# Additive mask bias written into PSUM by an identity product, logits in token order, and a regrouped schedule, in a fused attention and soft-MoE kernel

## Chip, cores and metric

The kernel runs on one core of a Trainium2 chip. The metric is the device time of one execution in microseconds (us); lower is better. Runs are sorted into fast and slow by their time, and each run lists the mean clock that was granted to TensorE (PE), as a share of full speed. Only fast runs are compared. The other engines are VectorE (DVE), ScalarE (ACT) and GpSimd (POOL). SBUF holds the operands here, PSUM (in banks) the sums of the products.

## The reference, cut to what matters

```python
# attention: B, H, S, D = 8, 8, 576, 64; heads 0-3 a plain window, heads 4-7 a dilated one
scores = scale * q @ k.T                           # scale = 1/8
mask_plain = (rel >= 0) & (rel < 32)
mask_dil   = (rel >= 0) & (rel < 128) & (rel % 4 == 0)
attn = softmax(where(mask, scores, -1e9)) @ v      # x: 4608 tokens x 512
# soft MoE: 32 slots, 8 experts of 4 slots, hidden size 1024
logits = x @ phi
slot_input = softmax(logits, axis=tokens).T @ x
slot_out[e] = relu(slot_input[e] @ w1[e]) @ w2[e]
out = softmax(logits, axis=slots) @ slot_out       # needs every expert
```

Inputs and outputs are fp32 in HBM. The loads cast to fp16 on their way into SBUF and the output stores cast back. q, k, v, w1 and w2 are 62 MB, the output 9.4 MB.

## The kernel before

One loop iteration handles one batch element ("a batch" below) and mixes three stages of a pipeline: scores, exponentials and plain products of batch b, dilated products and logits of b-1, slot sums of b-2. After the loop come the experts, which need all weights, and then the outputs, which need all experts. Scores are computed with 32 contraction rows (tiles of 32 rows by 128 columns of PE's 128x128 array, four at a time, one per head); the mask is a product on DVE after the exponential. `keep_busy` issues products with no use ("fillers"), meant to keep the clock of PE up.

```python
def emit_scores(b, st):                    # st 0, 1: plain and left edge; st 2: dilated
    tiles = [psum_s.tile([128, 2, 512], FP32, ...) for i in range(2)]   # 2 banks each
    ...
    for kt_, k0, qt_, q0, c0, w in jobs:
        for tt in range(2):
            for h in range(4):
                nc.tensor.matmul(tiles[h // 2][:, h % 2, c0 : c0 + w],
                    kt_[32 * h : 32 * h + 32, k0 : k0 + 128, tt],
                    qt_[32 * h : 32 * h + 32, q0 : q0 + w, tt],
                    start=(tt == 0), stop=(tt == 1), skip_group_check=True)
    return tiles

def emit_exp(b, st, tiles, i):             # ACT
    nc.scalar.activation(out=pt, in_=tiles[i][:, :, 0:n], func=AF.Exp, scale=SCALE)

def emit_mask(b, st, i):                   # DVE: 480, 304 or 512 columns x 2 heads
    nc.vector.tensor_tensor(out=pt, in0=pt, in1=MASK[st]..., op=ALU.mult)

def back_logits(b, rp, filler):            # rp: two of the four residues mod 4
    keep_busy(bank, filler, 512)
    for kc in range(4):
        if kc < 2:                         # plain half: every 4th column
            rhs = xTp_t[b][:, kc, :].rearrange("p (i r) -> p r i", r=DIL)[:, 2 * rp : 2 * rp + 2, :]
        else:                              # dilated half: contiguous
            rhs = xTd_t[b][:, kc - 2, 2 * rp : 2 * rp + 2, :]
        nc.tensor.matmul(lp, phi4[:, kc]..., rhs, start=(kc == 0), stop=(kc == 3))
    nc.scalar.activation(out=ET[...every 4th column...], in_=lp, func=AF.Exp, scale=1.0)
# ... cut: loads, transposes, products with v, normalisation on DVE, slot sums ...
```

Per batch the loop holds 4,000 columns of fillers: 2x224 after each of two transposes, 3x352 before the third normalisation, 3x512 and 1x512 before the logits.

The softmax here doesn't subtract the row's maximum and nothing guards it: scores larger than these inputs give would overflow.

## Time and profile before

| | before |
|---|---|
| time, median of 3 | 203.08 us (201.67 to 206.15) |
| profiled run | span 213.3 us, a slow run, mean clock 0.776 |
| batch period where the clock is 1.00 | 16.0 us |
| batch period where the clock is lower | 17.6 to 20.4 us |
| fp32 bytes read and written | 62.43 MB and 9.44 MB |

The page of the profile cuts the span into 40 equal slices (5.33 us each here). The digits are tenths: busy share of PE, granted clock, busy share of the DMA engines; the last row is what the DMA engines moved in GB/s, counted as fp16 for loads.

```profile
PE   7724999599988889999898898898689999758800
PEclk9965559955799965555999999999755699995555
DMA  5999999999994996699999999999999800199994
GB/s 120 164 205 208 206 205 212 209 205 165 202 210 64 202 205 120 107 196 212 210 185 198 211 209 207 209 171 181 206 207 207 140 5 0 35 404 406 409 407 114
```

Two things stand out. The clock falls to half, or near it, in stretches of three to five slices, in spite of the fillers. And the DMA engines move at most 205 to 212 GB/s of fp16, which is twice that in fp32 read.

The next view cuts the loop by the first exponential of the dilated scores, so that each row is one batch period. Columns: start and end, length, busy time (and count) of PE, PE weight loads, DVE, ACT and POOL, the granted clock, the DMA share and GB/s.

```profile
core 0: us, PE busy (x) PEld busy (x) DVE busy (x) ACT busy (x) POOL busy (x), PEclk, DMA share, GB/s
...
63.62:81.23 17.61, 15.91 (x271) 10.67 (x271) 14.65 (x37) 10.46 (x17) 7.00 (x8) 0.87 0.96 162
81.23:101.60 20.37, 20.37 (x271) 13.51 (x272) 14.18 (x34) 10.75 (x17) 7.42 (x9) 0.53 0.92 156
101.60:117.61 16.01, 14.23 (x271) 9.38 (x271) 13.88 (x35) 10.47 (x18) 10.12 (x12) 1.00 1.17 199
117.61:133.58 15.97, 14.21 (x271) 9.36 (x270) 13.87 (x35) 10.45 (x17) 3.49 (x4) 1.00 1.17 209
...
```

The run is slow, so its total is not compared with anything; the rows at clock 1.00 are. In such a row neither PE nor DVE is full by itself: they wait for each other. The timeline of these two rows (start, length, engine, line, operation, output<-inputs, partitions and elements, and in brackets the idle time before and what ended it) shows where, first for DVE and then for PE:

```profile
110.87 0.65 DVE L309 TENSOR_TENSOR p_0_0_1982<-p_0_0_1982,masks 128x960 f16<-128x960 f16 x1
...
112.53 0.67 DVE L309 TENSOR_TENSOR p_0_1_2001<-p_0_1_2001,masks 128x960 f16<-128x960 f16 x1
...
113.33 0.78 DVE L380 TENSOR_TENSOR rc_9_2074<-rc_9_2074,masks 128x4 f32<-128x4 f32 x1
```

```profile
114.63 0.28 PE L327 MATMUL o_1_2171<-v_93,p_0_0_1982 128*128 128x128 f16 x2 [0.28 <-DVE xd_2008 L381]
...
116.28 0.28 PE L327 MATMUL o_2_2187<-v_93,p_0_0_1982 128*128 128x128 f16 x2 [0.37 <-DVE xp_2167 L381]
...
120.19 0.81 PE L161 MATMUL lg_0_2286<-ones 128*128 128x512 f16 x3 [0.54 <-ACT xTd_2240 L417]
```

DVE spends 3.1 us of the 16 on six such mask products (by their start-to-start times) and 0.8 on one more small product, and PE waits for DVE's normalisations to free its output buffers. A filler of 512 columns costs PE 0.21 us.

### The profile page before, as it was taken

The page shows a single profiled execution, that of the slowest core. Times are in us where ns is not written, and L with a number is a line of the kernel's source. Part 1 is how long each engine was busy: PE and PEld are TensorE (multiplying, and loading weights), DVE is VectorE, ACT ScalarE, POOL GpSimd, SP SyncE. Part 2 cuts the span into 40 slices and gives each one's busy share as a digit, 9 for nine tenths or more (in the row PEclk, how much of TensorE's full clock was granted, in tenths as well). Part 3 has the DMA queues.
Part 4 walks back from the last instruction along what each step waited for, and adds up shares of the span by engine and source line. Part 5 has one row for each costly group of instructions (what it writes and reads, how often), then busy time and mean ns, then how long its engine had stood idle before and what let it go on. Part 6 is the DMA issues. An engine that isn't in the chain of part 4 may idle for free.

```text
span 213.3 us, 5627 instructions
## 1 busy us (share of the span) xinstructions
PE 173.7 (81%) x2410; PEld 102.3 (48%) x2410; DVE 133.5 (63%) x320; ACT 100.2 (47%) x160; POOL 86.5 (41%) x120
## 2 busy tenths in 40 slices
PE   7724999599988889999898898898689999758800
PEld 2312645474765566477556556556447554311100
DVE  3476892958599686668969969948225012545630
ACT  2033332553837825462783783784432502545520
POOL 7555644604441640633179005066200000297960
PEclk9965559955799965555999999999755699995555
DMA  5999999999994996699999999999999800199994
GB/s 120 164 205 208 206 205 212 209 205 165 202 210 64 202 205 120 107 196 212 210 185 198 211 209 207 209 171 181 206 207 207 140 5 0 35 404 406 409 407 114
DMA packets 32617, 41.27 MB, mean 193 GB/s; under 512 B 2128, under 2 KB 19664, under 8 KB 32592
## 3 DMA queue, kind: packets, MB, share of 16 engines
q0 software_dynamic: 32160, 40.41, 103.1%
q1 hardware_dynamic: 432, 0.50, 0.9%
q8 instruction: 19, 0.31, 0.5%
q14 instruction: 6, 0.05, 0.1%
HBM read 62.43 MB, written 9.44 MB: 337 GB/s over the span
## 4 chain that ended last, share of the span: by engine, by line
PE 49%; DVE 17%; DMA 9%; issue 9%; ACT 8%; POOL 4%; POOLq 0%; ACTq 0%
DMA raw_1_137<-in_k_dram 6%; POOL out_dram L770 4%; DMA raw_0_121<-in_q_dram 3%; PE warm_454 L161 3%; ACT ET L434 2%; PE so L725 2%; DVE qk_91 L258 2%; ACT v_93 L228 2%; DVE qk_90 L258 1%; DVE xd_2008 L381 1%; DVE xd_869 L381 1%; DVE xd_520 L381 1%; DVE xd_2381 L381 1%; PE hps_3298 L698 1%; PE hps_3299 L698 1%
## 5 line engine op out<-in xcount | busy, mean ns | idle before, releaser
L161 PEld LDWEIGHTS <-ones 128*128 128x128 f16 x138 | 12.4, 108 | 18.6 <-issue 10.8
L770 POOL DMA_DIRECT2D out_dram<-ot_3468 x1 | 0.6, 566 | 34.6 <-ACT ot_3468 L765 34.6
L431 PEld LDWEIGHTS <-phi_62 128*128 128x128 f16 x64 | 7.6, 119 | 9.1 <-issue 3.3
L290 PEld LDWEIGHTS <-qk_90 32*128 32x128 f16 x416 | 7.0, 103 | 10.0 <-issue 3.8
L762 PEld LDWEIGHTS <-ET 128*128 128x128 f16 x36 | 3.6, 99 | 15.4 <-issue 14.1
L161 PE MATMUL warm<-ones 128*128 128x512 f16 x26 | 7.5, 458 | 1.5 <-DVE ones L512 1.5
L290 PEld LDWEIGHTS <-qk_91 32*128 32x128 f16 x416 | 6.5, 98 | 3.0 <-issue 2.4
L161 PE MATMUL warm_454<-ones 128*128 128x512 f16 x20 | 5.8, 460 | 0.0
L487 DVE TENSOR_TENSOR UT<-UT,u_3264 128x160 f32<-128x160 f32 x1 | 0.3, 322 | 8.1 <-PE u_3264 L478 8.1
L304 ACT ACTIVATE p_0_0_238<-s_0_0_212 128x960 f16<-128x960 f32 x1 | 1.0, 972 | 9.1 <-PE s_0_1_213 L290 9.1
L205 PEld LDWEIGHTS <-onehot 32*128 32x128 f16 x128 | 3.3, 108 | 3.9 <-issue 3.4
L234 POOL COPY v_93<-vs_1950 128x1024 f16<-128x1024 f16 x1 | 1.0, 1037 | 9.8 <-PE o_8_2412 L327 9.8
L290 PE MATMUL s_1_0_245<-qk_90 32*128 32x16 f16 (+3 forms) x24 | 1.1, 208 | 4.6 <-DVE qk_90 L267 3.5
L214 PEld LDWEIGHTS <-onehot 16*128 16x128 f16 x32 | 3.8, 119 | 1.2
L251 POOL DMA_DIRECT2D w_3_2704<-in_moe_w_dram x1 | 0.9, 878 | 8.5 <-DVE qk_91 L267 8.5
L258 DVE STREAM_TRANSPOSE qk_90<-raw_0_121 128x576 uint32<-128x576 uint32 x1 | 1.3, 1258 | 4.8 <-DMA raw_0_121<-in_q_dram 4.8
L242 POOL COPY v_93<-v_93 32x1024 f16<-32x1024 f16 x4 | 4.1, 1034 | 0.2
L242 POOL COPY v_92<-v_92 32x1024 f16<-32x1024 f16 x4 | 4.1, 1034 | 0.2
L175 POOL DMA_DIRECT2D raw_6_1566<-in_q_dram x1 | 0.7, 696 | 8.5 <-DVE qk_90 L267 8.5
L175 POOL DMA_DIRECT2D raw_4_808<-in_q_dram x1 | 0.7, 701 | 7.9 <-DVE qk_90 L267 7.9
L478 PEld LDWEIGHTS <-ones 128*128 128x128 f16 (+1 forms) x40 | 3.4, 97 | 0.7 <-issue 0.7
L251 POOL DMA_DIRECT2D w_7_2833<-in_moe_w_dram x4 | 2.8, 717 | 2.0 <-ACT xTp_2776 L404 2.0
(1101 smaller groups left out, 658.2 us busy)
## 6 DMA issues: line engine op xcount, KB each, us to landing
w_0_76<-in_moe_w_dram POOLq DMA_DIRECT2D x1, 1024.0 KB, 16.7
w_1_77<-in_moe_w_dram POOLq DMA_DIRECT2D x1, 1024.0 KB, 18.9
w_2_78<-in_moe_w_dram POOLq DMA_DIRECT2D x1, 1024.0 KB, 12.8
w_3_79<-in_moe_w_dram POOLq DMA_DIRECT2D x1, 1024.0 KB, 12.9
w_4_80<-in_moe_w_dram POOLq DMA_DIRECT2D x1, 1024.0 KB, 12.8
w_5_81<-in_moe_w_dram POOLq DMA_DIRECT2D x1, 1024.0 KB, 17.0
w_6_82<-in_moe_w_dram POOLq DMA_DIRECT2D x1, 1024.0 KB, 12.5
w_7_83<-in_moe_w_dram POOLq DMA_DIRECT2D x1, 1024.0 KB, 17.2
```

The costliest lines, as they stand in the source:

```text
L161: nc.tensor.matmul(dst, ones[:, 0:128], ones[:, 0:width], start=True, stop=True, skip_group_check=True)
L214: nc.tensor.matmul(tiles[0][:, 0, 1, :], onehot[0:LEFT, r, :], vl[0:LEFT, 0:4, D * r : D * r + D], start=False, stop=(r == DIL - 1), skip_ ...
L228: nc.scalar.copy(out=dst[:, :, :, 0:D], in_=src.rearrange("p t (h d) -> p t h d", h=4))
L242: nc.gpsimd.tensor_copy(out=vL[b % NV][0:32, :, :, 0:D], in_=vD[b % NV][96:128, :, :, 0:D])
L258: nc.vector.transpose(out=dst, in_=src)
L290: nc.tensor.matmul(tiles[h // 2][:, h % 2, c0 : c0 + w], kt_[32 * h : 32 * h + 32, k0 : k0 + 128, tt], qt_[32 * h : 32 * h + 32, q0 : q0 + ...
L381: nc.vector.tensor_tensor(out=dst.rearrange("p (u d) -> p u d", u=4), in0=o[0:nq, :, 0:D], in1=rc[0:nq, :, None].broadcast_to([nq, 4, D]), ...
L431: nc.tensor.matmul(lp, phi4[:, kc].rearrange("p c s -> p (c s)"), rhs, start=(kc == 0), stop=(kc == 3))
L434: nc.scalar.activation(out=ET[:, b * S : b * S + S].rearrange("p (i r) -> p r i", r=DIL)[:, 2 * rp : 2 * rp + 2, :], in_=lp, func=AF.Exp, ...
L698: nc.tensor.matmul(hps[fc][32 * j : 32 * j + 32, :], siTm[:, dc, e, :], w1t[e][:, dc, 512 * fc : 512 * fc + 512], start=(g == 0 and dc == ...
L725: nc.tensor.matmul(so[32 * j : 32 * j + 32, :], hTm[g][:, c, 32 * j : 32 * j + 32], w2t[4 * g + j][:, c, :], start=(seen[j] == 0), stop=(s ...
L770: nc.gpsimd.dma_start(out=out[r0 : r0 + 128, :], in_=ot)
```

## The change

The intent is to take the mask off DVE. A product of the 128x128 identity with a table of 0 and -60000 writes the bias into the score banks first, and the scores accumulate on it; after the scale of 1/8 the exponential of a masked score is 0. The Trainium skill, "PSUM — Partial Sum Buffer" (The four PSUM rules), names this way of starting an accumulation from a value: put the seed through the PE by an identity product. The PE time for it is to be paid by dropping the fillers in the loop and by an explicit order of operations that changes the tile size of the array less often (15 changes per batch). The logits now run in token order, the last 64 rows of v come by a DMA of their own instead of a permuting product, one of two v evictions moves from ACT to DVE, and the first-layer weights are issued somewhat earlier. The small product with `mask_ok` (the 0.8 us on DVE) is dropped too.

```diff
+FAR = -60000.0
-    m.append(ok)
-    return np.ascontiguousarray(np.concatenate(m, axis=1).astype(np.float16))
+    return np.ascontiguousarray(np.where(np.concatenate(m, axis=1), 0.0, FAR).astype(np.float16))
+ORDER = """
+SA D0 nD0 XP0 eXP0 eA1 D2 XP1 loads D3 eA0 nD2 EP ER nD3 QP0 DL last eXP1 D1 SB eB0 nDL nD1
+P1 VS eB1 U P2 UA R2 R1 QD00 nP1 nP2 SC eC0 eC1 P0 nP0 XD0 XD1 eXD0 QP1 P3 eXD1 P4 R3 R4
+QD01 VP VE0 VE1 QD10 LG0 LG1 nP3 ET0 ET1 nP4 QD11
+"""
     def emit_scores(b, st):
+        n, m0 = WIDTH[st], BIAS0[st]
+        for h in range(4):
+            nc.tensor.matmul(
+                tiles[h // 2][:, h % 2, 0:n], ident, bias[:, m0 : m0 + n],
+                start=True, stop=False, skip_group_check=True)
...
-                        start=(tt == 0),
+                        start=False,
-    def emit_mask(b, st, i):
...
-        keep_busy(bank[:, 288:512], 2, 224)        # and the other fillers of the loop
...
-                rhs = xTp_t[b][:, kc, :].rearrange("p (i r) -> p r i", r=DIL)[:, 2 * rp : 2 * rp + 2, :]
+                rhs = xTp_t[b][:, kc, n * hf : n * hf + n]
-                rhs = xTd_t[b][:, kc - 2, 2 * rp : 2 * rp + 2, :]
+                rhs = xTd_t[b][:, kc - 2].rearrange("p r i -> p i r")[
+                    :, n // DIL * hf : n // DIL * (hf + 1), :]
...  (cut: v tail by its own DMA, evictions, weight issue (1,1,1,1,2,2) -> (2,1,2,1,1,1))
```

In ORDER, S is scores, eA to eC their exponentials (ET those of the logits; eX are evictions of transposes), P and D products with v of the same block (plain, dilated), R products with the block before (32x32 array tiles), n normalisations, X transposes, LG logits, EP and U the slot sums, QP and QD transposes of q and k, VP and VE the permutation and eviction of v. Each engine runs its own items in that order.

## The prediction

> **What bounds it now.** The profile is of a slow run (213.3 us, mean granted clock 0.776); the timed runs are at 203.08. In the chain of waits the eight batches repeat. From mask to mask a batch takes 15.99 us at clock 1.00 (110.95 to 126.95, 126.95 to 142.94), and 17 to 19.6 where the clock row shows 0.5 to 0.8; those excesses sum to about 9.5 us, so I take the timed runs as mostly warm. In a warm batch (timeline) DVE has one hole, about 1.6 us, before the first dilated normalisation; PE stands idle about 1.4 us (0.16, 0.28, 0.37, 0.54), each time for DVE or ACT. The chain hops between PE and DVE; neither alone is the bound. After the loop: row sums, experts, then outputs at 406 GB/s, about 27 us from the first (184) to the end. Loads run at 205 to 212 GB/s and end near 170 in this slow run: a second limit not far below.
>
> **Costs per warm batch, by start-to-start times in the timeline.**
> - DVE loses six mask products (0.57, 0.60, 0.39, 0.39, 0.59, 0.60 = 3.1 us) and the validity product (0.8), and gains one V eviction (0.5 to 0.6): 14.4 us of work becomes about 11.1.
> - PE gains 12 identity products, 4x(480+304+512) = 5,184 columns. The warm 512-column filler is 0.21 us apart, so 2.15 us. It loses fillers of 4,000 columns (1.65 us), the 16-row permutation (0.45), and tile-size switches: I count 23 before and 15 after. A switch costs 0.1 us beyond a matmul (114.80 to 114.96 against 0.055), 0.8 us together. "TensorEngine Tiling (Array Packing)" of the Trainium skill (Key Properties) says changing the tiling mode drains the engine; the trace agrees. Strided logit operands (0.25 us a matmul against 0.18 contiguous here) move from the plain to the dilated half: a wash. PE work goes from 14.6 to about 13.8 us.
> - ACT loses one V eviction (0.5), and the exponentials of the logits write contiguously (0.8 us now for 288 columns, about 0.45 expected): 10.4 becomes about 9.
> - POOL issues one more small DMA (0.55 us); not critical.
>
> **What reaches the time.** With the masks gone the products wait for ACT alone, and PE becomes the leading engine; its remaining waits (buffers of the outputs, the copies before the logits) I put at 0.5 to 0.9 us. A batch takes about 14.4 us, 1.6 less. Seven repeat fully: 11 us. The first batch gains 1 to 2, because the second transpose of batch 1, which waits for k until 21.5 us, now stands behind three normalisations. The last back end and the fillers of the warm-up change by under 1 us. The limit from loads: 62.4 MB read at about 415 GB/s of fp32 is 150 us, plus the last expert pieces and 27 us of output: about 184. Sum: 203 - 11 - 1.5 - 1 = about 189.5.
>
> **Prediction: 189 us, 8 in 10 between 183.5 and 197.** Faster by over 2%: 0.90; within 2%: 0.07; slower: 0.03.
>
> **What would show it.** Batch period 14 to 15 us at clock 1.00; DVE busy per period about 10.5 to 11.5 against 13.9, with new holes; identity products about 2.1 us a batch at 0.2 us each; logit exponentials near 0.45 us; no fillers in the middle and a granted clock no lower; gap between last load and first output shrunk.
>
> **What would make it wrong.** A clock that falls to half without the fillers: then a batch takes 18 us and the gain is gone. The strided dilated logits costing more than 0.3 us each. Identity products that wait for score buffers, putting evictions on PE's path. Loads: if a batch nears 14 us the last weights set the end and nothing below 184 is reachable.

## The result, and the profile after

| | before | after |
|---|---|---|
| time, median | 204.62 us of 4 (201.67 to 210.81) | 190.73 us of 4 (190.48 to 191.67) |
| ratio of fast runs | | 0.943 (95%: 0.936 to 0.951) |
| mean clock, profiled run | 0.776 (slow run) | 0.880 (fast run) |
| batch period at clock 1.00 | 16.0 us | 14.0 us |
| DVE busy in it | 13.9 us | 10.7 us |

A ratio is the mean time of one kernel's fast runs over that of the other's fast runs of the same rounds, so it is not quite the ratio of the medians: here 190.9 over 202.4, the mean of 201.67 and 203.08. The other two runs of before are slow. The outputs are right.

The page after, in slices of 4.72 us:

```profile
PE   6951999999999999999999998998899957869300
PEclk9995557999999999999999999999985999975555
DMA  5999999999999999999999999999999990999992
GB/s 136 191 203 209 203 205 205 211 213 206 205 212 206 206 215 209 206 208 209 205 209 212 201 211 209 203 208 209 205 208 208 208 167 15 302 408 403 409 407 76
```

After the first batch the clock stays up (1.00 in the six batch periods after the first, 0.84 in the first; it dips again in the last iteration, which has no scores), and the DMA row has no hole between the first slice and the one at 15 GB/s: the loads run at their highest rate from start to end. The chain of waits, followed back from the last instruction, goes over loads nearly everywhere:

```profile
DMA 76%; POOL 9%; issue 8%; DVE 2%; PE 1%; POOLq 0%; ACT 0%; DVEq 0%
```

The same batch windows as before:

```profile
core 0: us, PE busy (x) PEld busy (x) DVE busy (x) ACT busy (x) POOL busy (x), PEclk, DMA share, GB/s
...
70.66:84.67 14.01, 13.79 (x269) 8.98 (x268) 10.73 (x28) 8.93 (x16) 4.14 (x6) 1.00 1.20 208
84.67:98.67 14.00, 13.78 (x269) 8.97 (x268) 10.74 (x28) 8.94 (x17) 7.25 (x10) 1.00 1.20 208
...
```

PE now leads: it is busy for 13.8 of 14.0 us, DVE for 10.7. In the timeline of a batch, the identity products, the logits and their exponential:

```profile
96.96 0.60 PE L282 MATMUL s_2_0_2174<-bias,ident 128*128 128x512 f16 x2
97.41 0.59 PE L282 MATMUL s_2_1_2175<-bias,ident 128*128 128x512 f16 x2
...
101.35 0.42 PE L452 MATMUL lg_0_2282<-xTp_1977,phi_62 128*128 128x288 f16 x2
101.61 1.14 PE L452 MATMUL lg_0_2282<-xTd_2236,phi_62 128*128 128x288 f16 x2
102.57 0.42 PE L452 MATMUL lg_1_2287<-xTp_1977,phi_62 128*128 128x288 f16 x2
```

From 96.96 to the first score at 97.93 the four identity products of 512 columns take 0.97 us; the other two groups take 0.92 and 0.77 (a wait of 0.22 left out), so 2.66 us per batch with the entry to the scores, against 2.15 predicted. The logits hold a surprise: from 101.35 to 101.61 two contiguous products take 0.26 us, and from 101.61 to 102.57 two strided ones take 0.96 us, or 0.48 us each.

After the loop, PE waits for the last expert weights, though the loads never paused:

```profile
152.68 0.38 PE L746 MATMUL so<-w_6_2734,hslab 128*32 128x512 f16 x1 [0.72 <-DMA w_6_2734<-in_moe_w_dram]
153.94 0.38 PE L746 MATMUL so<-w_7_2782,hslab 128*32 128x512 f16 x1 [0.88 <-DMA w_7_2782<-in_moe_w_dram]
155.19 0.38 PE L746 MATMUL so<-w_7_2782,hslab 128*32 128x512 f16 x1 [0.63 <-DMA w_7_2782<-in_moe_w_dram]
```

So the time seems to have moved from one limit to another: from an attention loop that PE and DVE shared, with a clock that fell, to a loop led by PE that ends just before the loads do. Every part of that sentence can be tested, and was.

### The profile page after: what moved, and what is told of

It is laid out like the page before. It is cut to its first block, busy times and chain, and to the rows that moved or that the text cites. A ratio compares the mean times of both kernels' runs of the same rounds, so it can differ in the third digit from the quotient of the medians.

```text
span 188.9 us, 5560 instructions
## 1 busy us (share of the span) xinstructions
PE 158.4 (84%) x2392; PEld 88.9 (47%) x2392; DVE 109.6 (58%) x287; ACT 87.2 (46%) x152; POOL 90.1 (48%) x128
## 4 chain that ended last, share of the span: by engine, by line
DMA 76%; POOL 9%; issue 8%; DVE 2%; PE 1%; POOLq 0%; ACT 0%; DVEq 0%
DMA w_7_2782<-in_moe_w_dram 14%; DMA w_2_86<-in_moe_w_dram 13%; DMA w_2_78<-in_moe_w_dram 11%; DMA vs_1258<-in_v_dram 11%; DMA raw_7_1992<-in_q_dram 10%; DMA vs_147<-in_v_dram 6%; DMA vs_135<-in_v_dram 4%; DMA out_dram<-ot_3501 3%; DMA out_dram<-ot_3546 2%; DMA out_dram<-ot_3441 2%; POOL out_dram L791 1%; POOL v_93 L236 1%; POOL v_93 L240 1%; POOL v_93 L244 1%; POOL vs_562 L199 0%
## 5 line engine op out<-in xcount | busy, mean ns | idle before, releaser
L282 PEld LDWEIGHTS <-ident 128*128 128x128 f16 x96 | 8.8, 101 | 18.1 <-issue 13.2
L170 PEld LDWEIGHTS <-ones 128*128 128x128 f16 x56 | 6.2, 118 | 10.5 <-issue 6.1
L452 PEld LDWEIGHTS <-phi_62 128*128 128x128 f16 x64 | 6.1, 101 | 9.4 <-issue 7.6
L170 PE MATMUL warm<-ones 128*128 128x512 f16 x26 | 8.5, 503 | 1.5 <-DVE ones L541 1.5
L302 PEld LDWEIGHTS <-qk_90 32*128 32x128 f16 x416 | 6.1, 98 | 4.9 <-issue 4.9
L302 PEld LDWEIGHTS <-qk_91 32*128 32x128 f16 x416 | 5.6, 92 | 4.3 <-issue 4.3
L253 POOL DMA_DIRECT2D w_7_2782<-in_moe_w_dram x4 | 2.8, 711 | 7.1 <-DMA w_2_86<-in_moe_w_dram 4.4
L170 PE MATMUL rs<-ones 128*128 128x448 f16 x10 | 4.3, 569 | 0.0
L746 PEld LDWEIGHTS <-hslab 128*32 128x32 f16 x64 | 1.7, 95 | 4.9 <-issue 3.7
L282 PE MATMUL s_1_1_294<-bias,ident 128*128 128x304 f16 x2 | 0.7, 434 | 4.0 <-DVE v_92 L229 4.0
L746 PE MATMUL so<-w_7_2782,hslab 128*32 128x512 f16 x8 | 2.4, 379 | 1.7 <-DMA w_7_2782<-in_moe_w_dram 1.5
```

The lines of the kernel that those rows point to most:

```text
L170: nc.tensor.matmul(dst, ones[:, 0:128], ones[:, 0:width], start=True, stop=True, skip_group_check=True)
L253: nc.gpsimd.dma_start(out=w2t[e][:, n * i : n * i + n, :], in_=src[:, n * i : n * i + n, :])
L282: nc.tensor.matmul(tiles[h // 2][:, h % 2, 0:n], ident, bias[:, m0 : m0 + n], start=True, stop=False, skip_group_check=True,)
L302: nc.tensor.matmul(tiles[h // 2][:, h % 2, c0 : c0 + w], kt_[32 * h : 32 * h + 32, k0 : k0 + 128, tt], qt_[32 * h : 32 * h + 32, q0 : q0 + ...
L452: nc.tensor.matmul(bank[:, 0:n], phi4[:, kc].rearrange("p c s -> p (c s)"), rhs, start=(kc == 0), stop=(kc == 3),)
L746: nc.tensor.matmul(so[32 * j : 32 * j + 32, :], hTm[g][:, c, 32 * j : 32 * j + 32], w2t[4 * g + j][:, c, :], start=(seen[j] == 0), stop=(s ...
```

## The experiments

The main theory (A): moving the masks off DVE and the dense schedule are both needed; the identity products cost PE what they save DVE unless fillers, waits and switches are taken out. Rivals: DVE alone was the bound (B); the fillers alone cost the time (C); the order alone gains it (D). Twelve kernels ran, on three chips. On the first chip the kernel before had a median of 207.88 us, on the second 207.0, on the third 205.56, because many of its runs there were slow (mean clock 0.78 to 0.88; fastest run 200.6). So a ratio depends on the runs of before that it is set against: the same two kernels give 0.943 in the result and 0.927 in e8. Ratios are given where enough fast runs of both exist.

### e1: identity products in the kernel before

```diff
 # kernel before, emit_scores: bias products first, scores accumulate; all mask products dropped
+        for h in range(4):
+            nc.tensor.matmul(tiles[h // 2][:, h % 2, 0:n], ident, masks[:, m0 : m0 + n], start=True, ...)
-                        start=(tt == 0),
+                        start=False,
-            emit_mask(b, 0, 0)     # and the five others
```

Expected: 

> The kernel before with one part of the change: identity products write the bias, the mask products on DVE are gone; order, fillers, logits as before. Theory A (the gain comes from order, switches and fillers, which only pay for the identity products): PE work per warm batch goes from about 13.4 us (16.0 less 2.6 of waits) to about 16.1, so the period cannot fall: 16.2 to 17.5 us, time 203 to 213. Theory B (DVE was the bound and moving the masks off it is the gain): period about 14.5, time about 192.

Measured: 204.38 us median (fast runs 203.41 to 204.65), ratio 0.992 (0.980 to 1.004), unclear at best. Two of its batch periods (the profiled run, 207.96 us, counts as slow, but these rows are at clock 1.00):

```profile
46.93:63.72 16.79, 15.83 (x284) 10.26 (x283) 11.36 (x28) 10.54 (x17) 6.70 (x8) 1.00 0.98 164
63.72:80.34 16.62, 15.66 (x284) 10.35 (x283) 10.78 (x28) 10.55 (x17) 6.70 (x8) 1.00 1.02 170
```

Theory A is kept, B falls: taking 2.5 us of work off DVE made the warm period longer, 16.6 to 16.8 instead of 16.0. But the clock reads 1.00 in all six periods after the first one, which the kernel before does not reach. The fast runs have a mean clock of 0.906 to 0.924, those of before on this chip 0.82 to 0.855: the steadier clock seems to give back about what the longer period costs.

### e2 and e3: fillers out, with and without the identity products

```diff
-        keep_busy(bank[:, 288:512], 2, 224)
-                keep_busy(ubank[:, 160:512], 3, 352)
-        keep_busy(bank, filler, 512)
```

Expected of e2 (e1 without the loop's fillers): 

> As e1, and the fillers in the loop are gone too. Theory A: PE work about 14.3 us and waits of 1 to 1.8 left by the old order: period 15.3 to 16, time 196 to 203. Theory B: 190 to 192, all of the gain. If the clock falls without fillers, time above 205 with PE clock 0.5 stretches.

Measured: 199.52 us median (196.62 to 202.03), ratio 0.962 (0.940 to 0.984). Periods at clock 1.00 are 15.5 and 16.0 us, those at 0.90 are 16.6.

```profile
43.43:58.91 15.48, 14.13 (x273) 9.43 (x271) 10.76 (x28) 10.54 (x17) 6.70 (x8) 1.00 1.20 208
58.91:75.50 16.59, 15.27 (x273) 10.01 (x271) 11.01 (x28) 10.54 (x18) 6.70 (x8) 0.90 1.11 189
```

That is A's range: identity products paid by the fillers gain part of the whole change (ratio 0.962 against 0.943 or 0.927), though at the 2% threshold unclear. PE still stands idle 1.35 us of the 15.48, and the clock dips. What separates e2 from the kernel after is the order together with the logits, the v tail, the v eviction and the dropped small product; these were not taken apart further than e9 and e10 do.

Expected of e3 (kernel before, only the fillers taken out): 

> The kernel before without the fillers in the loop, nothing else. Theory A: the fillers stand partly in PE's waits for DVE, so taking away 1.76 us of them shortens the warm period by less than 0.6 us (15.4 to 16.0), and the clock falls to 0.5 more often: time 203 to 215. Theory C (the fillers themselves cost the gain): period 14.3, time about 191.

Measured: 208.45 us median (204.51 to 212.0); only one of its four runs counts as fast, so no ratio. The mean clock of its runs is 0.66 to 0.73. One of its periods (in a slow run):

```profile
82.47:100.68 18.21, 17.71 (x260) 12.50 (x260) 14.16 (x35) 10.55 (x18) 7.64 (x9) 0.50 0.92 154
```

C falls: without fillers and without identity products PE has less work than in before, e1 or e2, and runs it at a lower clock. What the fillers were worth in the kernel before is not shown: the one fast run (204.51 us) lies with the fast runs of before on this chip (204.83 to 207.88).

### e4 and e5: masks back on DVE in the kernel after, then with the identity products kept as dead weight

```diff
 # e4: kernel after, ORDER gets mask products (mA..mC), no identity products
-... nD3 QP0 DL ...   nP1 nP2 SC ...            QD01 VP VE0 VE1 QD10 ... nP4 QD11
+... nD3 QP0 mA1 mA0 DL ... nP1 nP2 mB0 mB1 SC ... QD01 VP VE0 VE1 mC0 QD10 ... nP4 mC1 QD11
 # e5: as e4, but the 12 products of ident and the 0/1 table stay; the scores overwrite them
-                        start=False,
+                        start=(tt == 0),
```

Expected of e4: 

> The changed kernel with the mask products back on DVE and no identity products; everything else of the change kept. PE work per batch about 10.6 us, DVE about 14.2. Theory A (both parts are needed: PE paid by order, DVE relieved by the bias): DVE leads, period 14.3 to 15.7, time 193 to 201. Theory D (the order is all, the bias gives nothing): 188 to 191, equal to the changed kernel. A clock that falls without dense products shows as 0.5 to 0.8 in the clock row and more than 200.

Measured: 206.36 us median (205.64 to 207.73), ratio 1.004 (0.993 to 1.015): the whole gain is gone. This missed the range of A (193 to 201) and lies where the expectation put a fallen clock. The mean clock is 0.70 to 0.72:

```profile
61.69:80.42 18.73, 16.14 (x256) 11.81 (x256) 14.89 (x35) 8.94 (x16) 8.19 (x9) 0.59 1.18 209
80.42:96.12 15.70, 13.78 (x256) 9.79 (x257) 13.78 (x35) 8.94 (x17) 7.32 (x9) 0.83 1.14 186
```

Is that the clock, or DVE? e5 keeps PE's load as in the kernel after and DVE's as in e4. Expected: 

> As e4 (mask products on DVE in the changed kernel), but the identity products stay on PE at their old size and place, without effect: the scores overwrite them. PE work is that of the changed kernel, DVE that of e4. e4 ran at a mean clock of 0.70 to 0.72 and gained nothing. Theory E (the identity products' use is twofold: DVE relief and a clock that stays at 1.00): clock back at 1.00 in the loop, period 14.9 to 16 set by DVE, time 196 to 203. Theory F (e4 lost by the clock alone, DVE relief is worth nothing): time 190 to 192. Theory G (e4 lost by DVE alone): time stays at 204 to 208.

Measured: 202.75 us median (201.7 to 204.89), ratio 0.981 (0.970 to 0.993), inside E's range of time, but not its clock: E had 1.00 throughout the loop.

```profile
63.37:78.24 14.87, 13.79 (x268) 8.96 (x268) 13.38 (x34) 8.93 (x17) 7.50 (x9) 1.00 1.13 212
78.24:95.22 16.98, 15.89 (x268) 10.04 (x268) 14.36 (x36) 8.93 (x17) 7.32 (x9) 0.83 1.24 206
```

At clock 1.00 the period is 14.9 us, about 0.9 us more than in the kernel after: PE does the same work (13.8 us) and waits 0.86 us at one place for a normalisation on DVE. The rest comes from periods like the second line: while PE waits for DVE, the clock dips although all the dense products are there. From e4 to e5 the products are worth about 4 us (on two chips, so only roughly), and from e5 to the kernel after, with DVE relieved, another 11 (fast runs 201.7 to 203.25 against 190.85 to 191.67, same chip). D falls: the order without bias and without fillers gains nothing (e4), and with dead products in the place of fillers little (e5); the order with the old fillers was not run. F and G fall too.

### e6, e7, e8: loads, fillers, control

```diff
 # e6: experts 6 and 7 use the second-layer weights of 4 and 5 (wrong on purpose): 4 MB less in SBUF
-            load_w2(6)
+            w2t[6] = w2t[4]
-            load_w2(7, 4)
+            w2t[7] = w2t[5]
 # e7: fillers back, before each half of the logits
+        keep_busy(bank, 4, 512)
 # e8: the kernel after, unchanged
```

Expected of e6: 

> The changed kernel without the last two 2 MB weight loads (experts 6 and 7 use the second-layer weights of 4 and 5: wrong result on purpose). The loads then end about 10 us earlier. PE waited for the last weights for 0.7 + 0.9 + 0.6 + 0.3 us in the tail. Theory H (loads and computation end together): 188 to 189.3, a gain of 1.5 to 3 us and no more. Theory I (bound by loads throughout, as the chain of waits reads): about 181. Theory J (bound by computation, the loads merely abut): 190.5 to 191.

Measured: 186.42 us median (185.19 to 186.97), a wrong result as intended. Against e8 on the same chip (191.24) that is 4.8 us less. This is more than H's 1.5 to 3 us, and half of what I (bound by loads throughout) claimed; J (no gain) falls as well. The tail shows most of it: from the last slot sums on DVE to its copy of the slot outputs the kernel after takes 14.8 us (143.99 to 158.78), e6 11.1 us (142.62 to 153.72), with no wait for weights. First the kernel after, then e6:

```profile
143.99 0.32 DVE L516 TENSOR_TENSOR UT<-UT,u_3212 128x160 f32<-128x160 f32 x1 [7.88 <-PE u_3212 L507]
158.78 0.42 DVE L770 CAST so_sb<-so 128x256 f16<-128x256 f32 x1 [1.51 <-ACT so_sb L769]
142.62 0.32 DVE L516 TENSOR_TENSOR UT<-UT,u 128x160 f32<-128x160 f32 x1 [7.89 <-PE u L507]
153.72 0.42 DVE L768 CAST so_sb<-so 128x256 f16<-128x256 f32 x1 [1.01 <-ACT so_sb L767]
```

So loads cost 3.7 us at the end, not the 2.5 that the single waits sum to. Without these two loads the computation sets the end, 4 to 5 us earlier. A chain that reads "DMA 76%" did not mean that 76% of the time could be saved there.

Expected of e7: 

> The changed kernel with 4 fillers of 512 columns before each half of the logits, 4,096 columns or 1.75 us of PE work per batch, about what the kernel before had. If PE is the engine that sets the 14.0 us period: period 15.4 to 15.8, and with 2 us of slack in front of the last loads, time 198 to 202. If loads set the period: 14.0 to 14.3, time 190.5 to 192.

Measured: 196.71 us median (196.58 to 200.16; one of five is slow). PE sets the period:

```profile
57.85:73.58 15.73, 15.51 (x277) 9.76 (x276) 10.72 (x28) 8.93 (x17) 7.30 (x9) 1.00 1.20 209
```

The period grew by 1.72 us for 1.75 us of fillers, so there is no slack for fillers in the loop. The total grew by 5.5 us, less than the 7 or more expected (198 to 202 us). The trace shows where the difference went: from the last slot sums to the slot outputs e7 takes 9.9 us (158.01 to 167.94), against 14.8 in the kernel after. It no longer waits for weights (3.7 us, where I had allowed for 2), and the last batch, which has no scores and so no identity products, ran at full clock (9.9 against e6's 11.1).

Expected of e8: 

> The changed kernel unchanged, as a control on the same chip: 190.5 to 191.7, clock 1.00 in every batch period, period 14.0 us.

Measured: 191.24 us median (190.85 to 191.67), ratio 0.927 (0.919 to 0.935) to two fast runs of before; periods 14.00 us at clock 1.00 after the first, which is at 0.83. The control holds.

### e9 and e10: the tile sizes, and the order of the logits

```diff
 # e9, ORDER: two products of the block before go back behind their own block, four more switches
-P1 VS eB1 U P2 UA R2 R1 ...   P3 eXD1 P4 R3 R4
+P1 R1 VS eB1 U P2 UA R2 ...   P3 R3 eXD1 P4 R4
 # e10: logits as in the kernel before
-                rhs = xTp_t[b][:, kc, n * hf : n * hf + n]
+                rhs = xTp_t[b][:, kc, :].rearrange("p (i r) -> p r i", r=DIL)[:, 2 * hf : 2 * hf + 2, :]
 # ... likewise the dilated half (contiguous again) and the strided write of the exponentials
```

Expected of e9: 

> The changed kernel with the products of the previous block (32x32 array tiles) put back directly behind the products of their own block, for blocks 1, 3 (2 and 4 stay): four more switches of the array tile size per batch. If a switch costs 0.1 us as the trace of the kernel before reads: period 14.3 to 14.5 instead of 14.0, about 2.8 us over seven periods, which the 3.7 us that the tail waits for its last weights take up: time 190.5 to 192. If switches are free: period 14.0. If grouping is what keeps the clock: clock below 1.00 in the loop and time over 195.

Measured: 191.69 us median (190.75 to 192.22).

```profile
54.55:68.75 14.20, 13.98 (x269) 8.94 (x268) 10.74 (x28) 8.93 (x17) 7.63 (x10) 1.00 1.20 207
```

The period is 14.20 instead of 14.00, so four switches cost 0.20 us: about 0.05 us each, half of what I had read in the trace of before. The total did not move by more than the runs scatter (another chip than e8's). Grouping is real but small, and here it is hidden by the loads.

Expected of e10: 

> The changed kernel with the logits in the order of the kernel before (strided plain operand, contiguous dilated operand, strided write of the exponentials). The dilated products of the changed kernel took 0.48 us each against 0.13 for the plain ones, which the prediction had called a wash. Expected: products of 0.25 and 0.13 us, PE 0.9 us less per batch, exponentials 0.82 us instead of 0.41 on ACT; period 13.2 to 13.7 if PE leads, 14.0 or more if ACT is then in the way. Time 190 to 191.5 in either case, because the loads end where they end; 187 if computation were the bound.

Measured: 192.26 us median (192.08 to 192.46), above the 190 to 191.5 expected, and the most telling miss. The period is shorter, as expected and more, and the kernel is not faster; it is a little slower than e8's range, though on another chip:

```profile
53.81:66.88 13.07, 12.86 (x269) 8.99 (x268) 10.74 (x28) 9.60 (x16) 6.70 (x9) 1.00 1.21 207
66.88:84.98 18.10, 15.04 (x268) 10.10 (x267) 10.99 (x28) 9.60 (x17) 7.46 (x10) 0.79 1.19 209
84.98:99.02 14.04, 13.82 (x269) 10.04 (x268) 10.73 (x28) 9.78 (x17) 7.23 (x10) 0.90 1.21 209
```

The token order of the change therefore costs 0.93 us of each period. But two periods of 13.07 us run ahead of the loads, and the next batch has to wait for its q; the chain of waits of e10 has it:

```profile
57.16 20.45 DMA raw<-in_q_dram
77.61 0.02 issue
77.63 1.26 DVE qk L260
```

While it waits the clock falls, and that period takes 18.1 us. The tail shows the same once more:

```profile
153.04 0.58 PE L742 MATMUL so<-w,hslab 128*32 128x512 f16 x1 [4.75 <-DMA w<-in_moe_w_dram]
```

The last wait for weights ends at almost the same time as in the kernel after (155.5 against 155.2 us), so the loads are not late. But the longest of these waits is 4.75 us instead of 0.88, the clock from 155.2 to 160.3 us is 0.59 instead of 1.00, and the slot outputs are copied at 160.34 instead of 158.78 us. e9, on e10's chip, lies between: 1.92 us, 0.71, 159.60 us. The loads end where they end; a loop faster than they are only changes the place of the wait, and pays for it with the clock.

### e11 and e12: outputs that start while the last weights load

If loads are the limit, the part to attack is the pause of the DMA engines between loads and outputs (the slice at 15 GB/s). e11 loads the second-layer weights of the last two experts by output columns and writes the first ten output blocks by half rows, so that the first half of the columns is on its way out while the weights of the second half land. For this the expert products and row sums come in another order too. e12 adds fillers in the last batch.

```diff
 # e11 (kernel after)
-            load_w2(6)
+            load_w2_half(6, 0)
-            load_w2(7, 4)
+            load_w2_half(7, 0); load_w2_half(6, 1); load_w2_half(7, 1)
+    expert_out(0, (0, 1, 2, 3)); expert_out(1, (0, 1, 2, 3)); expert_out(0, (4, 5, 6, 7))
+    nc.vector.tensor_copy(out=so_sb[:, 0:256], in_=so[0])
+    out_half(0)                                  # blocks 0-9, columns 0-255
+    expert_out(1, (4, 5, 6, 7))
+    nc.scalar.copy(out=so_sb[:, 256:512], in_=so[1])
+    out_half(1)                                  # then the whole rows of blocks 10-35
 # e12: also, in logits()
+        if b == B - 1:
+            keep_busy(bank, 2, 512)
```

Expected of e11: 

> A version meant to beat both: the second-layer weights of the last two experts are loaded by output columns, and the first ten output blocks are written by half rows, so that outputs start while the last weights still load, and the 5 us in which the DMA engines stand nearly idle (the two slices at 167 and 15 GB/s in the changed kernel) go. If loads are the bound: 186.5 to 189 us. If the tail's computation is the bound: 190 or more.

Measured: 188.75 us median of 6 (187.73 to 189.63), correct.

```profile
DMA  5999999999999999999999999999999999999993
GB/s 122 201 201 212 201 206 203 212 214 208 202 213 209 203 212 216 205 202 212 207 205 214 205 203 208 207 209 206 208 209 205 199 198 183 226 387 409 408 406 108
```

The hole is gone: no slice from the second to the next to last is under 183 GB/s. On the same chip e9 ran at 191.69 and e10 at 192.26, and the fast runs of the kernel after, in the result and in e8, at 190.5 to 191.7. Every run of e11 is below these, by about 2 us or 1%. The kernel after itself was not on that chip, and too few fast runs of before were there for a ratio (its fastest took 200.6), so this is likely.

Expected of e12: 

> As e11, with two fillers of 512 columns before each half of the logits of the last batch only, where the clock of the changed kernel falls to 0.5 to 0.8 because no scores and so no identity products are left. 0.9 us of fillers against about 1.2 us of faster tail (e7 against e6, from the last slot sums to the slot outputs 9.9 against 11.1 us): 186 to 188.5, within 1 us of e11.

Measured: 188.7 us median of 6 (187.73 to 188.91), the same as e11 and 0.2 us above the range expected. A warmer clock in the last batch gains nothing while the loads are still coming.

## Why the prediction was right

The time was right (189 predicted, 190.73 measured, inside the range), the mechanism in its main line too, but with sizes that were off in both directions and partly cancelled. So the closeness of the total is partly luck. An estimate from the numbers below: against the sum of 189.5, seven periods of 14.0 instead of 14.4 give 2.8 us back, the first batch costs 1.3 more, the loads 3.7, in all 191.7. Two of the things that the prediction named as making it wrong did happen: strided logits above 0.3 us each, and last weights that set the end.

- "A batch takes about 14.4 us": 14.0. "DVE busy per period about 10.5 to 11.5": 10.7. "Logit exponentials near 0.45 us": 0.41. "A granted clock no lower": 0.84 in the first period, where before (a slow run) had 0.76, and 1.00 in the six that follow. e1, e4 and e5 show that neither half of the change carries this alone. PE waited 1.35 us per batch before (0.16, 0.28, 0.37, 0.54 in one period) and 0.22 after; the order and the lighter DVE took these out.
- "So I take the timed runs as mostly warm": only in part. The runs of before whose clock is listed have means of 0.78 to 0.88, and between the fast ones the time goes with it (207.88 us at 0.82, 204.83 at 0.855, 200.6 at 0.882). Part of the gain is that the clock no longer falls. How much in the fast runs is not measured, because the one profiled run of before is a slow one; this stays open.
- "Strided logit operands move from the plain to the dilated half: a wash": wrong. The dilated ones step over 144 elements and cost 0.48 us each, where the plain ones with a step of 4 had cost 0.25. e10 puts the price at 0.93 us a batch.
- "A switch costs 0.1 us": 0.05 (e9), so, as an estimate, the five fewer that the traces show (20 and 15) save about 0.25 us, not the 0.8 of eight. "About 2.15 us" of identity products is 2.66 with their entry into the scores. These two and the logits made PE's saving smaller than I thought; fewer waits made up for it.
- "The first batch gains 1 to 2": it gained 0.2. The first dilated exponential starts at 25.21 instead of 25.43 us (in the slow run of before). A new wait replaced the old: the v eviction that moved to DVE stands there behind a transpose that waits for q of batch 1, and the second scores of batch 0 wait 3.98 us for it:

```profile
19.07 0.67 PE L282 MATMUL s_1_1_294<-bias,ident 128*128 128x304 f16 x2 [3.98 <-DVE v_92 L229]
```

- "The limit from loads ... about 184": the term that was mis-sized most for the conclusion. The last weights were used at 157.75 us, about the 150 plus 7 of its sum, but 31.1 us of tail and output follow, not 27, so the limit is about 188.9 of span. e6 shows that it binds, for 4 to 5 us. In the sum of the prediction the loads bound nothing; in fact the loop is faster than predicted and the loads take the difference back.

## What to carry to other kernels

A cheaper instruction is worth what the engine order, the waits and the clock make of it: test each half of a change alone before crediting it. On PE, products that do something useful can take the place of fillers that only keep the clock up, if the engine also stops waiting for others. And before shortening a loop further, compare it with the time that its loads take: once the loads run without a hole, what is left to gain is a pause between them and the outputs, as in e11.

## What the Trainium skill lacked or had wrong

- "TensorE: Matmul & The Clock Gate", Part 1 (What's actually happening): it gives the full clock after about 3.4 us of sustained activity and the half clock after an idle window of about that length. Here PE's products were busy for all of a 20.4 us period at a mean clock of 0.53 (before, 81.23 to 101.60), and in e4 the clock averaged 0.59 (61.69 to 80.42) while PE's longest wait after the first batch was 2.6 us. With 12 identity products on the full array per batch it was 1.00 after the first period in e1 and in the kernel after, but 0.83 to 1.00 in the e5 periods shown and 0.81 to 1.00 in e2, which have these products too. So busy time in the records did not decide the clock; what did is not settled by these runs. Other parts of that page name products that count less than others, which no run here tests.
- "SBUF — State Buffer", Door 1 (the note on cachelines): it lets 16-bit operands (it names bf16, this one is fp16) be strided by up to 8 elements for free. A moving operand of 288 columns took 0.13 us contiguous, 0.25 us with a step of 4 elements (before and e10) and 0.48 us with a step of 144.
- "TensorEngine Tiling (Array Packing)", Key Properties: it says that a change of tiling mode drains the engine, and gives no cost. e9 puts it at about 0.05 us per change.
- "DMA: Bandwidth & Descriptors", Where 436 GB/s comes from: it lets the HBM side bind at about 358 GB/s for one core. The loads here landed 207 GB/s of fp16, which is 414 GB/s of fp32 read, for over 140 us, near the 425 GB/s that its own table measures and that the "HBM Reference" gives for a core that streams alone.
- No page was found that says that work which hides under a load stream can cost time when it is made shorter: e10's period fell from 14.0 to 13.07 us, one wait for q with its fallen clock made a period of 18.1 us, and a longer wait for the last weights left the tail at a clock of 0.59 and its slot outputs 1.6 us later.
